# Five row chunks for the scale weights and a new order of the image transposes, in a fused diffusion-transformer block on one core

## The chip, the cores and the metric

The kernel runs on one core of a Trainium2 chip. The metric is device microseconds of one execution. An execution of the program is also profiled; the span of the profile is about 1.8 us shorter than the execution's own time. Timed comparisons interleave runs of a kernel with runs of the kernel before on the same chip.

## The reference, cut to what matters

The block takes 2 x 256 image tokens and 2 x 32 text tokens of width 1152, and a conditioning vector `c`. The part that matters here is the image side up to Q, K and V:

```python
mod_i = (_silu(c) @ wmod_img).reshape(B, 6, 1, D)
shi, sci, gai = mod_i[:, 0], mod_i[:, 1], mod_i[:, 2]
hi = _layernorm(x_img) * (1 + sci) + shi
qkvi = hi @ wqkv_img
# ... the same for text, joint attention over text and image tokens, output projection, gate, residual
```

There are 14 weight blocks of 1152 x 1152 in bf16 (2592 KB each), and each is read once.

## The kernel before: the parts that matter

All loads go out at the start on one queue, in the order in which they are wanted: the image rows, the scale block in three row pieces, the V block in four, then whole blocks, first the shift block and the query block.

```python
    SCC = (0, 4, K8, KT)                       # K8 = 8, KT = 9 rows of 128
    for r0, r1 in zip(SCC, SCC[1:]):
        nc.sync.dma_start(w_sc_i[:, r0:r1, :], sc_v[:, r0:r1, :])
    for r0, r1 in ((0, 1), (1, 3), (3, 6), (6, KT)):
        nc.sync.dma_start(w_v_i[:, r0:r1, :], v_v[:, r0:r1, :])
    w_sh_i = load_w(2, wmod_img, 0)
    w_q_i = load_w(3, wqkv_img, 0)
    # [cut: the other blocks]
```

V is computed from the normalised image rows times (1 + scale) alone (`hS_i`); the shift's part is added later. So V's first matmul needs three things: the transposed image rows, the complete scale vector `sc_ps` (81 matmuls of two columns, 9 for each row of the block), and row 0 of the V block. This is the order of work on TensorE:

```python
    x_transposes(0, 0)()          # 6 transposes of 128x128, then a copy to xT_i
    x_transposes(3, 0)()
    sc_cols(0, 4)                 # 36 scale matmuls
    x_transposes(6, 0)()
    warm_up(3)                    # 3 matmuls of 128x512 on zeros, to fill TensorE's time
    x_transposes(0, 1)()
    out31 = x_transposes(3, 1)    # its copy to xT_i is issued later
    out61 = x_transposes(6, 1)
    sc_cols(4, K8)
    warm_up(3)
    sc_cols(K8, KT)
    out31()
    out61()
    pin(nc.vector.tensor_scalar_add(sc1_i[:], sc_ps[:], 1.0))
    x_scale(0, 3, 0)              # hS_i = xT_i * (1 + scale), 3 blocks of image 0
    x_scale(0, 3, 1)
    # [cut: further scalings]
    v_open(A0, 0, 3)              # V: rows 0..2 into four PSUM banks
    v_open(A1, 0, 3)              # and into two more
    # [cut: rest of V, then the shift block: rows4(w_sh_i), the modulation, two more V banks]
    qk_img(w_q_i, 0, {1: (v_last, shift_v_rows), ...})   # query; V's last columns come after group 0
```

In the profiles `sc_ps` are the scale matmuls, `tp` the transposes, `wps` the warm-ups, `vps` is V, `gps` the shift block, and `ps` with the weights `t<-in_wqkv_img_dram` the query block. (In a profile of V or of the query, `t` is the weight tile.)

## Time and profile before

| | before |
|---|---|
| time, median of 3 | 123.43 us (123.36 to 123.49) |
| the profiled execution's own time | 124.34 us |
| span of the profile | 122.6 us |
| TensorE busy | 116.0 us (95%) |
| DMA | about 410 GB/s until 97 us |
| mean granted clock in the profile | 0.986 |

These are lines of the page of the kernel before. The digits are tenths, one for each fortieth of the span (3.06 us).

```profile
span 122.6 us, 2691 instructions
...
PE   5977979999999999999999999999999999999990
...
PEclk9998699999999999999999999999999999999999
```

TensorE is busy throughout except in the first six slices and at the very end. The granted clock is full except in the fourth and fifth slices (8 and 6 tenths).

This is the chain of waits of the kernel before, in order of time: start, duration, what ran or was waited for.

```profile
1.63 8.74 DMA t<-in_wmod_img_dram
...
10.42 1.07 PE sc_ps L61 x36
11.48 0.66 PE tp L64 x6
12.15 1.28 PE wps L61 x3
13.43 1.64 PE tp L64 x18
15.06 0.88 PE sc_ps L61 x36
15.94 0.67 PE wps L61 x3
16.61 0.22 PE sc_ps L61 x9
...
16.85 0.19 DVE sc_i L274
...
17.13 0.30 DVE hS_i L222
...
17.48 11.83 PE vps L61 x54
29.31 1.41 PE gps L61 x45
...
34.73 1.94 PE ps L61 x9
```

V starts at 17.48 us and from there TensorE never waits. Three warm-ups take 1.28 us at 12.15 and 0.67 us at 15.94. The first three ran at a granted clock of 0.50. The stretch table (busy time of each engine in a window, then granted clock, DMA share, GB/s) says where that stretch lies:

```profile
7.80:11.21 3.41, 1.96 (x46) 1.47 (x45) 3.00 (x8) 3.31 (x9) 0.00 (x0) 1.00 1.03 385
11.21:14.62 3.41, 3.41 (x34) 2.58 (x31) 1.46 (x3) 2.31 (x5) 0.00 (x0) 0.50 1.04 405
```

The landing of a load is its issue plus its time to landing. The query block is issued at 11.80 us in this trace. This is the table of DMA issues in the window from 8 to 17 us (size, then microseconds to landing):

```profile
t<-in_wqkv_img_dram SPq DMA_DIRECT2D x1, 2592.0 KB, 21.5
```

So the query weights land at 33.3 us, and the first query matmul starts at 34.57 us.

### The profile page before, as it was taken

How to read it: one execution, taken by the hardware profiler on the slowest of the kernel's cores; microseconds unless marked ns; L12 is line 12 of the kernel's file. 1: busy time of each engine (PE TensorE's matmuls, PEld its weight loads, DVE VectorE, ACT ScalarE, POOL GpSimd, SP SyncE). 2: the span in 40 equal slices, each digit the busy share in tenths (PEclk: the TensorE clock that was granted, in tenths of full speed). 3: DMA queues.
4: the chain of work that ended last, by engine and by line, in shares of the span. 5: the costliest groups of instructions: out<-in, count | busy, mean ns of one | idle time of the engine just before them, and what ended most of it. 6: DMA issues, size and time to landing. Idle time of an engine off the chain costs nothing.

```text
span 122.6 us, 2691 instructions
## 1 busy us (share of the span) xinstructions
PE 116.0 (95%) x1154; PEld 69.1 (56%) x1154; DVE 56.1 (46%) x151; ACT 34.2 (28%) x72; POOL 14.4 (12%) x36
## 2 busy tenths in 40 slices
PE   5977979999999999999999999999999999999990
PEld 2336744445448444464545747567777766666660
DVE  1568347015862361212143122128776756666571
ACT  4799410005741131211111110211636730000000
POOL 7140000000000307000000000000030907100000
PEclk9998699999999999999999999999999999999999
DMA  4999999999999999999999999999999950411222
GB/s 120 375 388 389 408 407 410 411 412 413 410 381 399 415 400 411 397 407 410 408 413 411 410 406 413 417 399 412 414 406 405 405 200 24 144 42 54 102 48 96
DMA packets 18694, 41.03 MB, mean 335 GB/s; under 512 B 1027, under 2 KB 1563, under 8 KB 18683
## 3 DMA queue, kind: packets, MB, share of 16 engines
q1 hardware_dynamic: 17584, 39.56, 83.1%
q0 software_dynamic: 704, 1.05, 2.7%
q10 hardware_dynamic: 395, 0.26, 0.7%
q8 instruction: 9, 0.15, 0.4%
q14 instruction: 2, 0.02, 0.0%
HBM read 39.52 MB, written 1.34 MB: 333 GB/s over the span
## 4 chain that ended last, share of the span: by engine, by line
PE 88%; DMA 7%; DVE 1%; SPq 1%; issue 0%; DVEq 0%
PE ps L61 50%; PE vps L61 14%; DMA t<-in_wmod_img_dram 7%; PE gps L61 6%; PE aps L61 6%; PE sps L61 4%; PE tp L64 2%; PE sc_ps L61 2%; PE wps L61 2%; PE pT_ps L64 1%; SPq L97 1%; DVE tmp L579 1%; DVE o L580 0%; PE gT L64 0%; PE tpt L64 0%
## 5 line engine op out<-in xcount | busy, mean ns | idle before, releaser
L61 PE MATMUL ps<-xT_i,t 128*128 128x512 bf16 x162 | 36.5, 379 | 0.0
L61 PEld LDWEIGHTS <-t 128*128 128x128 bf16 x432 | 23.2, 97 | 19.5 <-DMA t<-in_wmod_img_dram 0.9
L61 PE MATMUL ps<-t,aT 128*128 128x384 bf16 (+3 forms) x153 | 20.2, 308 | 0.0
L61 PEld LDWEIGHTS <-aT 128*128 128x128 bf16 (+1 forms) x153 | 13.0, 101 | 7.1 <-issue 0.5
L61 PE MATMUL vps<-t,hS_i 128*128 128x512 bf16 x72 | 16.0, 379 | 0.7 <-DVE hS_i L222 0.7
L61 PEld LDWEIGHTS <-hS_i 128*128 128x128 bf16 x72 | 6.8, 97 | 8.6 <-DVE hS_i L222 0.8
L61 PE MATMUL wps<-warm 128*128 128x512 bf16 x29 | 9.1, 470 | 1.2 <-DVE warm L121 1.2
L579 DVE TENSOR_TENSOR tmp<-ps,gb 128x384 bf16<-128x384 f32 (+2 forms) x13 | 6.8, 527 | 6.4 <-PE ps L61 6.3
L157 ACT CAST qkT<-ps 128x512 bf16<-128x512 f32 (+1 forms) x6 | 3.4, 569 | 18.3 <-PE ps L61 18.3
L342 DVE TENSOR_SCALAR qkT<-ps 128x512 bf16<-128x512 f32 (+1 forms) x5 | 3.3, 665 | 10.6 <-PE ps L61 10.6
L155 DVE CAST qkT<-ps 128x512 bf16<-128x512 f32 (+1 forms) x5 | 3.1, 625 | 10.7 <-PE ps L61 10.6
L155 DVE CAST v_i<-vps 128x512 bf16<-128x512 f32 x5 | 3.4, 689 | 9.9 <-PE vps L61 9.9
L344 ACT ACTIVATE qkT<-ps 128x512 bf16<-128x512 f32 (+1 forms) x6 | 3.3, 553 | 14.3 <-PE ps L61 14.3
L451 POOL DMA_DIRECT2D mod_scratch<-g_sb x4 | 2.3, 588 | 40.9 <-ACT g_sb L157 40.9
L61 PE MATMUL aps<-pT,v_i 128*128 128x288 bf16 x36 | 6.7, 287 | 0.0
L61 PE MATMUL gps<-t,sT 128*32 128x256 bf16 (+1 forms) x180 | 6.1, 279 | 0.0
L61 PEld LDWEIGHTS <-warm 128*128 128x128 bf16 x29 | 3.0, 115 | 4.8 <-issue 1.9
L551 DVE TENSOR_SCALAR aT<-aps,sv_i 128x288 bf16<-128x288 f32 x9 | 4.7, 517 | 2.4 <-PE aps L61 2.3
L157 ACT CAST v_i<-vps 128x512 bf16<-128x512 f32 x4 | 2.3, 580 | 12.3 <-PE vps L61 12.3
L61 PE MATMUL sps<-qkT 128*128 128x288 bf16 (+1 forms) x54 | 5.5, 287 | 0.0
L61 PEld LDWEIGHTS <-sT 128*32 128x32 bf16 x180 | 4.3, 96 | 1.8 <-issue 1.5
L553 ACT ACTIVATE aT<-aps,sv_i 128x288 bf16<-128x288 f32 x9 | 4.5, 501 | 2.5 <-PE aps L61 2.5
(100 smaller groups left out, 117.1 us busy)
## 6 DMA issues: line engine op xcount, KB each, us to landing
t<-in_wmod_txt_dram SPq DMA_DIRECT2D x3, 2592.0 KB, 17.7
t<-in_wqkv_txt_dram SPq DMA_DIRECT2D x3, 2592.0 KB, 13.6
t<-in_wmod_img_dram SPq DMA_DIRECT2D x2, 2592.0 KB, 19.8
t<-in_wqkv_img_dram SPq DMA_DIRECT2D x2, 2592.0 KB, 22.4
t<-in_wo_img_dram SPq DMA_DIRECT2D x1, 2592.0 KB, 15.9
t<-in_wo_txt_dram SPq DMA_DIRECT2D x1, 2592.0 KB, 17.7
t<-in_wmod_img_dram SPq DMA_DIRECT2D x2, 1152.0 KB, 10.0
t<-in_wqkv_img_dram SPq DMA_DIRECT2D x2, 864.0 KB, 14.7
```

The lines of the kernel that those rows point to most:

```text
L61: return pin(nc.tensor.matmul(*a, **k))
L64: return pin(nc.tensor.transpose(*a, **k))
L97: nc.sync.dma_start(x_i[:, b * TPB:(b + 1) * TPB, :], x_img[b].rearrange("(p t) d -> p t d", t=TPB))
L155: nc.vector.tensor_copy(out_ap, in_ap)
L157: nc.scalar.copy(out_ap, in_ap)
L342: nc.vector.tensor_scalar_mul(out_ap, in_ap, SCALE)
L344: nc.scalar.mul(out_ap, in_ap, SCALE)
L451: nc.gpsimd.dma_start(gsc[si, b, :].rearrange("(g j) -> g j", g=NGG), g_sb[b:P:32, :])
L551: nc.vector.tensor_scalar(dst, aps[:], bias, None, op0=ALU.add)
L553: nc.scalar.activation(dst, aps[:], ACT.Identity, bias=bias)
L579: nc.vector.tensor_mul(tmp[:, 0:n], ps[:, 0:n], gb[:, b, c0:c0 + n])
```

## The change

The intent: give each scale piece its matmuls as it lands, between the transposes, so that the last row (landed at 14.01 us in the trace before) is followed by V at once.

```diff
-    SCC = (0, 4, K8, KT)
+    SCC = (0, 3, 5, 7, K8, KT)
@@
     x_transposes(3, 0)()
-    sc_cols(0, 4)
     x_transposes(6, 0)()
+    sc_cols(0, 3)
     warm_up(3)
+    sc_cols(3, 5)
+    warm_up(1)
+    sc_cols(5, 7)
     x_transposes(0, 1)()
     out31 = x_transposes(3, 1)
+    sc_cols(7, K8)
+    sc_cols(K8, KT)
     out61 = x_transposes(6, 1)
-    sc_cols(4, K8)
-    warm_up(3)
-    sc_cols(K8, KT)
-    out31()
     out61()
     pin(nc.vector.tensor_scalar_add(sc1_i[:], sc_ps[:], 1.0))
     x_scale(0, 3, 0)
     x_scale(0, 3, 1)
+    out31()
```

## The prediction

> **What bounds the kernel now.** The page gives TensorE 95% of a 122.6 us span. The chain of waits, read in order, is TensorE without a gap from 17.48 us (first V matmul) to 118.8 us. Before that it is: first scale-weight piece lands 10.37 (issued 1.63 + 8.74), 36 scale matmuls 1.07, 6 transposes 0.66, 3 warm-ups 1.28, 18 transposes 1.64, 36 scale matmuls 0.88, 3 warm-ups 0.67, 9 scale matmuls 0.22, then the VectorE tail (add 0.19, first scaling 0.30, gaps) to 17.48. The last scale piece, row 8, landed at 14.01 (issue plus time to landing), so V starts 3.5 us after its data: here TensorE's program order is the limit. The DMA engines carry about 410 GB/s until 97 us, so later weights have limited slack.
>
> **What changes, costed from that chain.**
> - The 6 transposes of block 6 of image 0 move before the first scale matmuls, into the 0.69 us idle before 10.42: -0.66 us of work on the chain.
> - Two warm-ups fewer: -0.4 us (the last three took 0.67).
> - The last 6 transposes are issued after the last scale matmuls and run under the VectorE tail (add plus first scaling, about 0.65 us): -0.4 us.
> - A first piece of three rows lands some 0.7 us earlier, but by then TensorE ends those 18 transposes at about 10.1: a further 0 to 0.3 us.
> - One VectorE copy (0.56) moves behind six scalings (0.2 each in a row); the second V group needs its bank only 12 matmuls (2.6 us) after V begins: no wait.
> - Two more DMA issues (about 0.5 us each on the queue) cost nothing: data is queued well ahead; landings of row 8 (14.0) and of the V weights (14.72, 16.16, 18.3, 20.47) should stay within 0.3 us.
>
> V should start near 15.9 us instead of 17.48, just enough for V rows 1-2 (16.16, needed 0.86 us after the start).
>
> **What gives part back.** Query weights landed at 33.34 us, by DMA rate alone; the first query matmul starts at 34.57. That slack is only 1.2 us, so of 1.6 us gained a wait on the query weights should take back about 0.4. The shift weights (landed 26.9, used 29.24) just suffice. Every later weight landed 3.7 us or more before use, so 1.2 us should reach the end.
>
> **Clock.** The stretch table shows the granted clock at 0.50 from 11.21 to 14.62, full around it: one 3.41 us stretch[...]. Before, TensorE was 1.96 us busy of 3.41 in the window ahead and lost full clock, then 3.41 of 3.41 and regained it. [...]
>
> **Predicted:** 122.2 us, 121.7 to 123.3. Faster by over 2%: 0.03; within 2%: 0.94; slower by over 2%: 0.03.
>
> **Right if:** first V matmul at 15.5 to 16.3 us; full clock from about 14.6; a new TensorE wait of 0.2 to 0.6 us on the query weights; everything after that shifted by about 1.2 us.
>
> **Wrong if:** clock is half beyond 14.6 (gain near 0); smaller pieces land later (V not before 16.5); V stalls on its weights; query weights do not land near 33.3.

The sum is 0.66 + 0.4 + 0.4 us and 0 to 0.3 us, about 1.6 us off V's start at 17.48 us (so 15.9); about 0.4 us of it goes to the wait for the query weights, and 123.43 less 1.2 us is 122.2 us. The clock risk stood beside the sum: about 15% that V would begin at half clock, for a loss of up to 1 us, which was the guess.

## The result, and the profile after

| | before | changed |
|---|---|---|
| time, median of 4 | 123.40 us (123.20 to 123.49) | 123.88 us (123.81 to 123.97) |
| ratio | | 1.0042 (95%: 1.0025 to 1.0059) |
| span of the profile | 122.6 us | 122.1 us |
| mean granted clock in the profile | 0.986 | 0.998 |

A ratio is the mean time of one kernel's fast runs over the mean of the other's fast runs of the same rounds. It is not quite the ratio of the medians quoted. Executions over 1.5% slower than the fastest of the same kernel are left out of the means.

The changed kernel is slower by 0.4% in time while its profile is 0.5 us shorter. First the page after, the same lines:

```profile
span 122.1 us, 2689 instructions
...
PE   5999899999599999999999999999999999999980
...
PEclk9999999999999999999999999999999999999999
```

No slice lost the clock. The 5 in the eleventh slice (from 30.5 us) is a new idle time of TensorE. Next TensorE in order of time in the changed kernel: start, duration, group, and in brackets an idle time before it with what ended it.

```profile
9.90 0.82 PE L61 MATMUL sc_ps<-sT,t 128*128 128x2 bf16 x27
...
13.22 0.72 PE L61 MATMUL sc_ps<-sT,t 128*128 128x2 bf16 x18
13.80 0.49 PE L64 MATMUL tp<-ident,xn_i 128*128 128x128 bf16 x6
14.60 1.04 PE L61 MATMUL vps<-t,hS_i 128*128 128x512 bf16 x4 [0.31 <-DVE hS_i L222]
15.79 10.95 PE L61 MATMUL vps<-t,hS_i 128*128 128x512 bf16 x50 [0.15 <-DMA t<-in_wqkv_img_dram]
26.75 1.17 PE L61 MATMUL gps<-t,sT 128*32 128x256 bf16 x36
...
33.71 2.12 PE L61 MATMUL ps<-xT_i,t 128*128 128x512 bf16 x9 [1.46 <-DMA t<-in_wqkv_img_dram]
```

The change did what it was meant to do. The last scale piece landed at 13.51 us, V started at 14.60 us, and V's work before the shift block ended at 26.75 us. Then the query group waited 1.46 us for its weights. The chain of waits of the changed kernel says it in two lines: what ended last goes back through the query weights to their issue, and V's start is not on the chain at all. (The step before their issue, at 12.06 us, is the landing of the third scale piece at 12.04. In both traces the DMA issues of the SyncE and ScalarE queues name eight completion semaphores, over and over; the query block's issue names that of the third scale piece and waited for its landing, 0.9 us after the issue before it had ended at 11.16 us. In the kernel before, with two loads fewer ahead, it names that of the first piece, landed at 10.37 us, and it went out at 11.80 us, when the issue before it had ended.)

```profile
12.06 21.60 DMA t<-in_wqkv_img_dram
...
33.71 2.12 PE ps L61 x9
```

One more pair of lines matters, from the waits of the issuing queue at the end of the program (waiter, what ended the wait, microseconds in total, times, longest). First the kernel before, then the changed one:

```profile
SPq L633 <- DMA out_dram<-o: 1.2, 3, 0.4
```

```profile
SPq L635 <- DMA out_dram<-o: 1.5, 1, 1.5
```

Before returning, the program checks the DMAs' semaphores in a fixed row (the eight stand in the same order in both traces, but for one number). Before, it met the last three outputs one after another as they landed. In the changed kernel the last output's semaphore is the first of the eight: the queue stands there 1.5 us and then has seven more checks to do, 0.06 us apart in the trace (before, there was one more). By the trace's semaphore events the last output landed 0.96 us before the end of the span before, and 1.33 us before the end after.

### The profile page after: what moved, and what is told of

It is laid out like the page before. It is cut to its first block, busy times and chain, and to the rows that moved or that the text cites. A ratio compares the mean times of both kernels' runs of the same rounds, so it can differ in the third digit from the quotient of the medians.

```text
span 122.1 us, 2689 instructions
## 1 busy us (share of the span) xinstructions
PE 115.0 (94%) x1152; PEld 67.9 (56%) x1152; DVE 56.1 (46%) x151; ACT 34.2 (28%) x72; POOL 14.3 (12%) x36
## 4 chain that ended last, share of the span: by engine, by line
PE 69%; DMA 25%; SPq 2%; DVE 1%; issue 0%
PE ps L61 51%; DMA t<-in_wqkv_img_dram 18%; DMA t<-in_wmod_img_dram 8%; PE aps L61 6%; PE gps L61 5%; PE sps L61 4%; PE vps L61 2%; SPq L101 1%; PE pT_ps L64 1%; SPq L97 1%; DVE tmp L581 1%; DVE o L582 0%; PE tpt L64 0%; PE gT L64 0%
## 5 line engine op out<-in xcount | busy, mean ns | idle before, releaser
L61 PE MATMUL wps<-warm 128*128 128x512 bf16 x27 | 8.5, 468 | 1.2 <-DVE warm L121 1.2
L346 ACT ACTIVATE qkT<-ps 128x512 bf16<-128x512 f32 (+1 forms) x6 | 3.3, 553 | 15.9 <-PE ps L61 15.9
```

The source lines that it names most:

```text
L61: return pin(nc.tensor.matmul(*a, **k))
L346: nc.scalar.mul(out_ap, in_ap, SCALE)
```

## The experiments

Theory A has three parts. (1) The trace before was of an untypical execution with a half-clock stretch; at full clock the kernel before starts V near 15.9 us and already waits for the query weights. (2) So the earlier V of the changed kernel turns into a longer wait for the same weights. (3) The two extra DMAs shift the last output's semaphore to the front of the closing row, and that costs about 0.37 us.

Rival B: the smaller pieces or the extra issues slow the stream of weights, and the query weights land later. Rival C (formed on reading the result): V's earlier end lets the text input's load out earlier, ahead of the tail of the query weights, and delays them.

Fifteen runs were made, two of them of unchanged kernels. All gave correct results. "Query landing" below is the last of the 16 completion events of the query block in the profile; "ending" is from the last output's landing to the end of the span.

### 1. The kernel before, profiled again (`before_again`)

Edit: none.

> The kernel before, unchanged, looked at again. Theory A (the trace the prediction was read from was an untypical execution: its own time was 124.34 us beside 123.2 to 123.5 of the others, and it had the half-clock stretch at 11.2 to 14.6): a new profile at full clock shows a span of about 121.6 us, V starting near 15.9 instead of 17.48, a TensorE wait of 0.1 to 0.5 us before the first query matmul that ends with the landing of the query weights, and the query matmuls starting at 33.3 to 33.6. Theory B (smaller pieces or more DMA issues slow the stream of weights): V at about 17.5 and no wait on query weights in the kernel before even at full clock, query weights landing at 33.3 or sooner. The ratio to before should be 1.00.

Measured: ratio 1.0014 (0.9977 to 1.0051). The profiled execution took 123.37 us and its clock was full. The page and the TensorE timeline of this run:

```profile
span 121.6 us, 2691 instructions
...
PEclk9999999999999999999999999999999999999999
```

```profile
15.80 11.83 PE L61 MATMUL vps<-t,hS_i 128*128 128x512 bf16 x54 [0.67 <-DVE hS_i L222]
27.56 1.17 PE L61 MATMUL gps<-t,sT 128*32 128x256 bf16 x36
...
33.58 2.12 PE L61 MATMUL ps<-xT_i,t 128*128 128x512 bf16 x9 [0.53 <-DMA t<-in_wqkv_img_dram]
```

The same kernel as in the trace before: V at 15.80 us instead of 17.48, and a wait of 0.53 us for the query weights (landing 33.54) that the first trace did not have. Part 1 of theory A is shown; B expected no such wait. "Untypical" does not mean rare, however: the record gives each execution's mean granted clock, and in 9 of the 50 timed executions of the unchanged kernel before in runs 1 to 15 it was 0.986, as in the first trace (where the stretch of 3.41 us at 0.50 in a span of 122.6 us makes this mean). These nine took 123.72 to 124.25 us, the others 122.92 to 123.93 us. Against the trace of run 1 the changed kernel can be read at last: V's work ends 0.81 us earlier (26.75 against 27.56), the first query matmul comes 0.13 us later (33.71 against 33.58), the ending is 0.37 us longer. The sum, +0.50 us, is the difference of the two spans (122.07 against 121.57) and close to the +0.48 us of the medians.

### 2. Two tiny loads more (`before_two_tiny`)

```diff
     w_o_t = load_w(1, wo_txt, 0)
+    pad = const.tile([1, 2, 256], bf)
+    for k in range(2):
+        nc.sync.dma_start(pad[:, k, :], c[0:1, 0:256])
```

> The kernel before with two tiny loads (512 bytes each, never read) issued after the last weight load, nothing else. They shift every later DMA by two places in the ring of eight completion semaphores, as the two extra pieces of the change do. Theory A (part of the loss is the ending: the last output's semaphore is then the first of the closing row of waits, and eight further checks of 0.06 us follow its landing): +0.3 to +0.45 us against before, all of it between the last landing and the end of the span (0.94 us in the profile before, 1.3 in the one after). Theory B (extra pieces early in the stream): no change, within 0.1 us.

Measured: ratio 1.0020 (0.9990 to 1.0049), too wide to decide. The profile decides: ending 1.32 us instead of 0.96, and the span 0.29 us longer although the last output landed 0.07 us earlier than in run 1. (In the trace after, seven checks 0.06 us apart follow the wait for the last output, not eight.) Run 9 repeats it where the times can show it.

### 3. The changed kernel with its outputs' semaphores put back (`after_six_tiny`)

Edit: the same loads as in run 2, six of them, in the changed kernel (2 + 6 places make a whole turn of the eight semaphores that the traces show).

> The changed kernel with six such tiny loads, so that the semaphores of the outputs stand again where they stood in the kernel before. Theory A: about 0.37 us less than the changed kernel, so 0 to +0.15 us against before. Theory B: still +0.4 us against before.

Measured: ratio 1.0008 (0.9972 to 1.0045), ending 0.96 us. As theory A had it; B expected +0.4 us. Its profile fell on an execution of 124.25 us with a half-clock stretch of its own. Its timeline and its stretch table:

```profile
14.30 1.04 PE L61 MATMUL vps<-t,hS_i 128*128 128x512 bf16 x4 [0.31 <-DVE hS_i L225]
16.50 12.64 PE L61 MATMUL vps<-t,hS_i 128*128 128x512 bf16 x50 [1.16 <-DVE hS_i L225]
```

```profile
13.11:16.52 3.41, 1.95 (x30) 1.12 (x26) 3.01 (x14) 1.20 (x2) 0.00 (x0) 1.00 1.04 403
16.52:19.93 3.41, 3.41 (x9) 1.21 (x9) 1.52 (x8) 0.00 (x0) 0.00 (x0) 0.50 1.04 411
```

After four V matmuls TensorE waits 1.16 us. The bracket names VectorE's scaling, but the six scalings that these matmuls read had ended by 15.22 us; V rows 1 and 2 landed at 16.45 us, and that is what ended the wait. The 3.41 us with this wait (1.95 us busy) were followed by 3.41 us at a granted clock of 0.50. So the changed kernel can lose its clock too, at another place than the kernel before (16.52 us against 11.21).

### 4. V's last columns ahead of the first query group, in the changed kernel (`after_vfirst`)

```diff
-    qk_img(w_q_i, 0, {1: (v_last, shift_v_rows), ...})            # [cut: the other hooks, unchanged]
+    qk_img(w_q_i, 0, {0: (v_last,), 1: (shift_v_rows,), ...})
```

> The changed kernel with the last V column block (36 matmuls, about 2.0 us, independent of the query weights) moved ahead of the first query group instead of after it, where the changed kernel waits 1.46 us for the query weights. Theory A (V's gain turned into that wait): the wait is gone, the second query group and all after it come 1.3 to 1.5 us earlier, about 122.4 to 122.7 us: 0.7 to 1.1 us faster than before in spite of the longer ending. If the loss came from anything later than the query weights, it would stay at +0.4 us.

Measured: 122.64 us, ratio 0.9927 (0.9894 to 0.9961), inside the expected range. The profile fell on the one slow execution (124.43 us, half clock from 16.38), so it is not used for the time. With 2 us of other work in front of the query weights the kernel becomes faster than the kernel before, as part 2 of theory A has it. That the wait is gone is not shown at full clock by this run (the half-clock stretch of its profile hides the wait); run 8 shows it.

### 5. The changed kernel again (`after_again`)

Edit: none.

> The changed kernel, unchanged, on the chip of these runs. Theory A: V starts at 14.1 to 14.7 us, waits until about 15.8 to 16.4 for V rows 1 and 2, then, if the clock stays full, waits 1.0 to 1.5 us before the first query matmul for the query weights (landing 33.3 to 33.7); ending 1.33 us after the last landing. Time within -0.2 to +0.7% of before. [...] Theory B: query weights land at least 0.3 us later than in the kernel before run here.

Measured: 124.04 us (123.43 to 125.77), ratio 1.0044 (1.0008 to 1.0080; the execution of 125.77 us counts as slow and is left out of it), the same loss in other rounds. The profile is of an execution of 124.68 us at full clock:

```profile
27.05 1.17 PE L61 MATMUL gps<-t,sT 128*32 128x256 bf16 x36 [0.53 <-DMA t<-in_wmod_img_dram]
...
34.48 2.12 PE L61 MATMUL ps<-xT_i,t 128*128 128x512 bf16 x9 [1.94 <-DMA t<-in_wqkv_img_dram]
```

The query weights landed at 34.44 us, later than I had expected (33.3 to 33.7), and the whole execution is late by as much. Thirteen of the 16 completion events of that block were there by 32.40 us; the last came 2 us later. The first query matmul started at 34.48 us, after the slowest of the 16. That this one is late is no exception: in the profiles of all runs the last event of the query block came 0.7 to 2.0 us after the thirteenth.

### 6. V's last columns first, in the kernel before (`before_vfirst`)

Edit: as in run 4, in the kernel before.

> The kernel before with the last V column block ahead of the first query group. Theory A: at full clock the kernel before waits only 0.4 to 0.5 us for the query weights, so it gains no more than 0.5 us (0.2 to 0.5, about 122.9 to 123.2); the changed kernel with the same move had 122.64. In an execution with the half-clock stretch it gains nothing. Theory B has no opinion on this one; if the change had nothing to give at V, before with this move would equal the changed kernel with it.

Measured: 122.81 us, ratio 0.9952 (0.9934 to 0.9970). That is 0.6 us, a little more than the 0.2 to 0.5 expected, because the wait varies with the landing. The waits of TensorE from 8 to 40 us in this run are one line:

```profile
PE vps L61 <- DVE hS_i L222: 0.7, 1, 0.7
```

The query wait is gone (landing 33.65 us, first query matmul 34.98). The times now lie between 122.74 and 122.87 us, where the kernel before has 123.07 to 123.72 in the same rounds. So most of the kernel's scatter goes with the wait for the query weights.

### 7. The wait for V rows 1 and 2 filled (`after_filled`)

```diff
-    x_scale(0, 3, 0)
-    x_scale(0, 3, 1)
+    x_scale(0, 1, 0)
+    x_scale(0, 1, 1)
     out31()
+    x_scale(1, 3, 0)
+    x_scale(1, 3, 1)
@@
-    v_open(A0, 0, 3)
-    v_open(A1, 0, 3)
+    v_open(A0, 0, 1)
+    v_open(A1, 0, 1)
+    v_open(A0, 1, 3)
+    v_open(A1, 1, 3)
```

> The changed kernel with the wait for V rows 1 and 2 filled: the two matmuls of row 0 of the second V group go ahead of rows 1 and 2 (their scaling and their bank are ready by then). Theory of the clock stretch[...]: the wait falls to 0.3 to 0.8 us, the stretch of half clock near 16.4 appears in no profile and times of 124 us and above disappear; the query wait grows by as much as the V work moved up, to 1.4 to 1.9 us, so the fast runs stay where they were (within 0.2% of the changed kernel). If the stretch still appears with the wait shortened, the wait is not its only cause.

The theory meant is that the wait brings on the half-clock stretch, since the two came one after the other in run 3 (a wait of 1.16 us, then 0.50 of the clock from 16.52 us).

Measured: 123.81 us, ratio 1.0042 (1.0015 to 1.0069). The profile shows no wait inside V, no half-clock stretch, a query wait of 1.26 us, and a new wait of 0.52 us for the shift weights. The fast runs stayed where they were, as expected. One expectation failed: two executions still took 124.3 and 124.4 us. The record gives both a mean granted clock of 1.000, so they had no half-clock stretch: a time over 124 us is no proof of one. Run 5 shows that a late query landing makes such a time too; whether it made these two is not shown.

### 8. All of it together (`combined`)

Edit: runs 4 and 7, and the last two scale pieces joined:

```diff
-    SCC = (0, 3, 5, 7, K8, KT)
+    SCC = (0, 3, 5, 7, KT)
@@
-    sc_cols(7, K8)
-    sc_cols(K8, KT)
+    sc_cols(7, KT)
```

> The changed kernel with three things added: V's wait filled as in the run before this one, the last V column block ahead of the first query group, and the last two scale pieces joined again (four pieces), so that one DMA fewer puts the last output's semaphore at the end of the closing row of waits. Theory A: V complete about 1.2 us earlier than in the kernel before at full clock, no or nearly no wait on the query weights, ending 0.90 us after the last landing instead of 0.96 (before) or 1.33 (changed): 121.9 to 122.5 us, 0.9 to 1.3% under before. Should the shift weights (landing 26.7 to 27.1) now be waited for, the gain stops at about 0.8%.

Measured: 122.00 us (121.88 to 122.29), ratio 0.9885 (0.9864 to 0.9905): the version that beats both kernels. Two of its four waits of TensorE from 8 to 40 us (the other two, before V, are for the normalised rows and a scale piece), and its wait at the end:

```profile
PE gps L61 <- DMA t<-in_wmod_img_dram: 0.4, 1, 0.4
PE vps L61 <- DVE hS_i L222: 0.3, 1, 0.3
```

```profile
SPq L638 <- DMA out_dram<-o: 1.1, 3, 0.4
```

No query wait; ending 0.90 us. It now waits for the shift weights, as one of the expectations allowed. It is 0.8 us better than run 6, which has the same move without the change: with the query wait out of the way, the change is worth something. How much of the 0.8 us is the change's own is not shown: `combined` also has the filled wait of run 7, and 0.06 us of it is the ending (0.90 against 0.96).

### 9. The ending in times (`before_vfirst_tiny`)

Edit: run 6 with the two tiny loads of run 2.

> The kernel before with the last V block ahead of the query groups (its times spread over 0.13 us only, so a third of a microsecond can be seen in times), plus the two tiny unread loads after the last weight load that shift the outputs' semaphores by two places. Theory of the ending: 1.32 us from the last landing to the end of the span instead of 0.96, and about +0.36 us in time: 123.15 to 123.25 if before stands at 123.3, against 122.81 without the loads. If the loads cost nothing, 122.8.

Measured: five of six runs between 123.11 and 123.19 us, one 124.41; median 123.16 us against 122.81 in run 6 (another chip, where before had 123.32; here it had 123.29). That is +0.35 us, and the ending in the profile is 1.33 us against 0.96. The ratio, 1.0000 (0.9963 to 1.0037), includes the one long run, whose mean granted clock was 0.986, as in the first trace with its half-clock stretch. Part 3 of theory A is shown: two loads of 512 bytes that nobody reads cost 0.35 us.

### 10. The pieces alone (`before_split`)

```diff
-    SCC = (0, 4, K8, KT)
+    SCC = (0, 3, 5, 7, K8, KT)
```

(in the kernel before, its order of work kept)

> The kernel before in its own order of work, with only the scale block loaded in five pieces instead of three. Theory A: V starts where it did (15.8 at full clock), query weights land within the spread seen so far (33.3 to 34.4), ending 1.33: +0.3 to +0.4 us against before, all in the ending. Theory B (pieces slow the weight stream): query weights and all weights of the first 40 us land later than in any profile of the kernel before, 0.3 us or more, and the loss is 0.6 us or more.

Measured: 123.88 us, ratio 1.0038 (1.0004 to 1.0073), that is +0.47 us by the ratio. V at 15.57 us, query landing 33.92 us, ending 1.32 us. The loss lies between the two expectations, and its interval (0.05 to 0.9 us) admits both. The query weights of this one profile landed 0.27 us later than the latest of any profile of the three-piece kernels, where B had expected 0.3 us or more in all weights of the first 40 us; the shift weights were 0.05 us later than the latest. Over all profiles but that of run 11, B finds no support in the stream: the shift weights, which come just before the query weights, landed on average at 26.94 us with five pieces (8 profiles) and at 26.98 us with three (6 profiles).

### 11. One piece fewer in the changed kernel (`after_joined`)

Edit: the last one of run 8 alone.

> The changed kernel with its last two scale pieces joined (rows 7 and 8 in one), so one DMA fewer and the last output's semaphore last in the closing row. Theory A: ending 0.90 us, about 0.43 us less than the changed kernel, so -0.1 to +0.15 us against before; V starts at 14.5 to 14.9 and the query wait stays (1.0 us or more). Theory B: at or above +0.3 us.

Measured: ratio 1.0005 (0.9963 to 1.0048), as theory A expected and B did not. The profiled execution took 170.42 us at a mean granted clock of 0.661; it is left out of the ratio, and its trace is not used (but for the ending, 0.90 us). Run 15 gives a clean trace.

### 12. The text input's load a little later (`after_xt_late`)

```diff
-    pin(nc.scalar.dma_start(x_t[:], xt_flat[:, :]))
     v_open([(2, 1)], 4, KT)
     v_open([(3, 1)], 0, KT)
+    pin(nc.scalar.dma_start(x_t[:], xt_flat[:, :]))
```

> The changed kernel with the text input's load (144 KB, about 0.36 us of the stream at 410 GB/s) issued after the V groups instead of before them. Theory C (the change lets this load in 2.5 us earlier, ahead of the tail of the query weights, and delays them): query weights land 0.2 to 0.4 us sooner than in the changed kernel, and the time falls by as much, to +0.1 to +0.3 us against before. Theory A: no difference outside the spread of the landings, still +0.4 us against before.

Measured: ratio 1.0020 (0.9994 to 1.0047), query landing 33.37 us. This is what C expected, but the landing is within the scatter of the changed kernel's profiles and the interval reaches from nothing to the whole of the loss. C was neither shown nor excluded.

### 13 to 15. The text input's load after the first query group

```diff
-    pin(nc.scalar.dma_start(x_t[:], xt_flat[:, :]))
@@ in qk_img, in the loop over j
+            if blk == 0 and j == 1:
+                pin(nc.scalar.dma_start(x_t[:], xt_flat[:, :]))
```

In the kernel before (`before_xt_after_q`):

> The kernel before with the text input's load issued after the first query group, so after the query weights have landed. Theory C (that load takes part of the stream ahead of the tail of the query weights): query weights land at 33.3 to 33.45, the first query matmul follows at 33.4 to 33.5, and the spread of the fast runs falls from about 0.8 us to 0.3 or less, with a median 0.1 to 0.3 us under before. Otherwise: landings between 33.3 and 34.4 and the same spread and median as before.

In the changed kernel (`after_xt_after_q`):

> The changed kernel with the same move. Theory C: query weights at 33.3 to 33.45; the difference to the run above is the ending alone, 0.3 to 0.4 us. If the two extra pieces themselves delayed the weights, the difference would be 0.5 us or more, with query weights later than in the run above.

In the changed kernel with the last two pieces joined (`after_joined_xt`):

> The same with the last two scale pieces joined. Theory A with C: ending 0.90 us instead of 1.33; time equal to that of before_xt_after_q within 0.1 us (0.06 us less at best): V's earlier start is worth nothing as long as the query weights are waited for.

| run | ratio | query landing | ending |
|---|---|---|---|
| before_xt_after_q | 0.9999 (0.9975 to 1.0024) | 33.47 | 0.96 |
| after_xt_after_q | 1.0033 (1.0011 to 1.0056) | 33.76 | 1.32 |
| after_joined_xt | 0.9983 (0.9958 to 1.0007) | 33.20 | 0.90 |

C falls: with the load issued at 35.7 us, after the query weights had landed, the kernel before has the same time and the same spread (122.98 to 123.86 us), and the changed kernel still lands its query weights at 33.76. So the earlier landing of run 12 needs no cause beyond the scatter. C's premise was off as well: its 2.5 us came from the half-clock trace (issue at 31.36 us); against run 1 the change lets the load out 0.8 us earlier (28.88 against 29.68). The differences between these three kernels go the way of the ending. In the profile of the second one a half-clock stretch (0.50 for 3.41 us) began at 14.88 us, just as V started, and cost nothing: V finished in time for the query weights (first query matmul 33.81, without a wait).

### The sum of the runs

The changed kernel with the long ending was measured five times, as it stands or with a part that should not matter for the fast runs: 1.0042, 1.0044, 1.0042, 1.0020, 1.0033, on average 1.0036. With the ending repaired it was measured three times: 1.0008, 1.0005, 0.9983, on average 0.9999. The difference, 0.37% of 123.3 us or 0.46 us, agrees with the ending (0.37 us by six loads, 0.43 us by one piece fewer). The single ratios have intervals of 0.2 to 0.4% to either side, so a tenth of a microsecond more or less is not shown. To that accuracy the change is worth nothing apart from the ending, as long as the query weights are waited for.

Left open: why the last of the query block's 16 events comes 0.7 to 2.0 us after the thirteenth, and what makes this vary; and a possible delay of the query landing by the five pieces. They also hold back the issue of the query block, which waits for a semaphore that a scale piece frees (issue at 11.12 to 12.43 us in the profiles with five pieces, 10.66 to 11.80 with three). No run separates this from the scatter; the shift weights, issued at about 10 us instead of 6.3, landed no later. Their mean landing is 33.66 us in 8 profiles, against 33.46 us in 6 with three pieces, and the spread within each group is larger than that (33.31 to 34.44; 33.30 to 33.65).

## Why the prediction was wrong, point by point

The predicted time was 122.2 us and the measured one 123.88.

- **What bounds the kernel now: the baseline was wrong, and this is the step that failed.** "V starts at 17.48" and "that slack is only 1.2 us" were read from an execution with a half-clock stretch. That execution took 124.34 us, yet its slack was set against the median of 123.43. In a typical execution V starts at 15.80 us and the slack of the query weights is below zero: TensorE waits 0.5 us for them (run 1). So the term "1.2 us should reach the end" had in truth the value 0, as the query wait cap applied to both kernels. The prediction had the cap, and had it at the right place (33.3); it did not see that the kernel before stood at it as well. Against the first trace itself V started 2.88 us earlier, but the first query matmul only 0.86 us (33.71 against 34.57), because the weights landed at 33.66; with 0.37 us more in the ending this is the 0.48 us between the two spans.
- **V should start near 15.9 us.** It started at 14.60 us. The pieces of the sum were sized with durations of the half-clock stretch. At full clock the 12 transposes after the third piece took about 0.67 us. The gain against the typical kernel before is 1.20 us at V's start and 0.81 us at the shift block, because V then waits for its rows 1 and 2 (15.75 us).
- **V is just early enough not to stall on rows 1 and 2.** It stalled, for 0.15 us in the trace after and 1.16 us in run 3's, because V started earlier than predicted.
- **A new wait of 0.2 to 0.6 us on the query weights.** The mechanism was right; the size was 1.46 us. All of V's 0.81 us went into it. And "by DMA rate alone" is not what the traces show: in the first one 13 of the 16 events were in at 31.89 us, and the last came at 33.34.
- **Two more DMA issues cost nothing.** Wrong in a way that was not thought of: on the queue the query block's issue went out at 12.06 us instead of 11.80, and no cost of that is shown; but they cost 0.37 us at the end of the program, through the place of the last output's semaphore in the closing row of waits (runs 2, 3, 9, 11).
- **Landings within 0.3 us.** Row 8 landed 0.5 us earlier than in the first trace (13.51 against 14.01), the V pieces 0.1 to 0.5 us earlier, the query weights 0.3 us later. These are of the size of the scatter from run to run, which the prediction had no measure of.
- **The clock risk.** The place it named, 11.2 to 14.6 us, was wrong. In the profile after, the clock was full (1.00) from 5.60 to 121.66 us, when the matmuls were done. Where a half-clock stretch appeared in a kernel with the new order (runs 3, 4, 14), it began at 14.9 to 16.5 us.

## What to carry to other kernels

Before reading a trace as the baseline, set the profiled execution's own time and its row of granted clock beside the timed runs; if they differ by as much as the change is meant to gain, take another trace first. An earlier start is worth only what the next landing lets through, so put independent work in front of that landing in the same step (the move of V's last columns gave 0.5% without the change, and together with the change and its repairs 1.15%). Count the DMAs: where completion semaphores are reused in turn and checked in a fixed row at the end, the output that lands last should have its check last (here the ending took 0.90 or 0.96 us with its check late in the row, 1.32 or 1.33 us with its check first).

## What else the traces show, and what they leave open

- The clock. In four profiles a half-clock stretch began during the program's work: at 11.21 us in the first trace and at 16.52, 16.38 and 14.88 us in runs 3, 4 and 14. In the first trace and in runs 3 and 14 the 3.41 us from there had a mean of 0.50 of the clock. TensorE had been busy for 1.96, 1.95 and 2.71 us of the 3.41 us before. But in run 7 the 3.41 us from 7.80 us, with 2.63 us busy, were followed by 3.41 us at full clock. So busy time alone does not tell when the clock is lost; what does is not shown.
- One execution of run 11, on one core, had a mean granted clock of 0.661, a span of 168.6 us and a time of 170.42 us. Why is open.
- The landings. In the first trace the load of V's row 0 had its first event at 12.83 us, before the last one (14.01 us) of the scale piece issued ahead of it. For the 2592 KB query block of run 5, 13 of 16 events were in at 32.40 us and the last at 34.44.
- The closing row of semaphore checks: 0.06 us a check after the last landing, 0.90 to 1.33 us from there to the end of the span by the place of the last output's semaphore.
